# Polysketch attention with an RWKV channel mix on one core: instructions over two PSUM banks, q in rows of tokens, and a new order

## The chip, the cores and the metric

The kernel runs on one core of a Trainium2 chip. Its engines are TensorE (PE, with weight loads listed apart as PEld), VectorE (DVE), ScalarE (ACT) and GpSimd (POOL); SyncE (SP) issues transfers, and ACT can issue them too. Each engine has its own list of instructions and works through it in order; a semaphore holds an instruction until those it depends on are done. The metric is the time of one execution in device microseconds (us), as the median of several.

## The reference

```python
def phi(x):                                   # S1, S2: (8, 32)
    a = np.einsum('rd,bhsd->bhsr', S1, x)
    b = np.einsum('rd,bhsd->bhsr', S2, x)
    return np.einsum('bhsi,bhsj->bhsij', a, b).reshape(*x.shape[:-1], r * r)
q_p, k_p = phi(q), phi(k)                     # q, k, v: (4, 4, 1088, 32) fp32
kv  = np.einsum('bhsf,bhsd->bhfd', k_p, v)
z   = np.sum(k_p, axis=2)
num = np.einsum('bhsf,bhfd->bhsd', q_p, kv)
den = np.einsum('bhsf,bhf->bhs', q_p, z)[..., None] + 1e-06
x   = (num / den).transpose(0, 2, 1, 3).reshape(4, 1088, 128)

x_prev = x shifted by one token (zeros first)
xk = mu_k * x + (1 - mu_k) * x_prev
xr = mu_r * x + (1 - mu_r) * x_prev
k  = np.maximum(xk @ w_k, 0)                  # w_k: (128, 1024)
out = sigmoid(xr @ w_r) * ((k * k) @ w_v)     # w_v: (1024, 128)
```

## The kernel before

There are four batches, each with four heads of 32 channels, so that head and channel fill the 128 partitions. The steps of a batch are these, with the names and lines of the kernel before.

*k side.* `kin` arrives by a DMA (L188). DVE transposes it to `kT` (L345). PE multiplies by the sketches S1 and S2 in two groups of four matmuls, one into each of two banks (L352); DVE transposes each bank into `abT` (L363). POOL, or now and then DVE, forms the products `phk` in three parts (L370). PE sums them with `v` into one bank in 24 matmuls a third (L379 `kv`), DVE masks the result into `w` (L391), and a copy of it with its halves exchanged, `ws`, is made by a product and an ACT copy for batch 0 (L394, L396) and by two DMAs for the others.

*q side.* `qin` arrives in four DMAs, one for each head, with a descriptor of 64 floats for each two tokens (L191). DVE transposes it to `qT` in two parts, 9 and 8 of 17 token pairs (L414). For batches 0 to 2, PE expands qT by S1 and by S2 (L453 `ex`): a call fills four banks. The S1 half is copied to `a_sb` (L465, ACT or DVE), the S2 half is multiplied by it into `phq` (L471, DVE). In batch 3, the S1 side is a compact sketch instead (L427), copied to `ac` (L434), and spread by four DMAs (L441). PE then computes the denominator (L480 `den`), DVE transposes it to `dT` (L491), ACT adds the small constant (`rc`, L494), and DVE takes the reciprocal `rr` (L498) and transposes it back to `rT` (L499). The numerator (L524 `num`) fills two banks a half. In batches 0 and 3 it is copied to `r` (L533, ACT), and a product with a selection matrix spreads rT (L545 `pr`); in batches 1 and 2, rT is spread by DMAs into `r` (L506) instead. DVE multiplies both into `xT` (L557), which is x, transposed.

*Channel mix.* x is scaled by mu and by 1-mu into `y1` and `y2` (L578 ACT, or L580 DVE), in three column chunks of 384 or 320. POOL adds them to `xk` (L583) and casts x to `xbp` (L586). For each chunk PE makes eight products with w_k (L612 `up`), each in a bank; a ReLU reads the bank into `kr` (L615 ACT, or L617 DVE); `k2` is the square of two kr together (L619 DVE, or L621 ACT). PE forms the gate (L640) and the product with w_v (L645 `down`), ACT the sigmoid `sg` (L648), and DVE multiplies both to `o` (L660), which a DMA stores.

Nothing in the program decides the sequence at run time. Every step is recorded as a numbered operation in `_Plan`, and a string ORDER, written out by hand, gives the order in which they are issued. `.1` behind a number takes the operation's other engine; `*n` puts n idle matmuls ahead of it. A second string, BANKS, gives each PSUM tile one of the eight banks. In the kernel before each bank is a tile of its own:

```python
def ps(shape=(P, 512)):
    t = _Buf(psum, None, 1, list(shape), F32)
    banks.append(t)
...
for t, i in zip(banks, BANKS):
    t.tag = "bank" + i
```

Of the kernel before, what the change touches and what calls it, by code (L numbers as in the profile page):

```python
# [12 lines left out]
F32 = mybir.dt.float32  # L13
# [9 lines left out]
class _Buf:  # L23

    count = itertools.count()

# [41 lines left out]
def kernel(  # L68
# [32 lines left out]
    SWAP = (0,)  # L101
    EX = [(0, NT), (NT, HT - NT)]
# [29 lines left out]
    )  # L132
    BANKS = (
        "10320601237564456732171260706452721514346072564350474163403104553451731204621045574267462557760"
        "25730423132051303046722470571652361340720623431721132763066547546645512103661151574635771053521"
        "47770463501457403621720236421256"
# [13 lines left out]

    def ps(shape=(P, 512)):
        t = _Buf(psum, None, 1, list(shape), F32)
        banks.append(t)
        return t

# [9 lines left out]
    Sst = const.tile([R, 2, D], F32)  # L165
    idle = nc.const_aps.tensor(1.0, [P, 512], BF16)
    nc.scalar.dma_start(Sst[:, 0, :], S1)
    nc.scalar.dma_start(Sst[:, 1, :], S2)

# [30 lines left out]
    mu = const.tile([DM, 2], F32)  # L200
# [7 lines left out]
    for h in range(H):  # L208
        load_q(0, h)
# [8 lines left out]

# [3 lines left out]
    mask4 = const.tile([P, H, R], F32)  # L222
    nc.gpsimd.memset(mask4[:], 0.0)
    for h in range(H):
        nc.gpsimd.memset(mask4[32 * h:32 * h + 32, h, :], 1.0)
# [20 lines left out]
    pS = ps()  # L246
    sp_ = St[:].ap[0]
    Skb = const.tile([P, 2, H, R], F32)
# [4 lines left out]
    first_in = {nm: op("IN", 0, f"{nm}0", lambda: None) for nm in ("k", "K", "v", "q", "S")}  # L253
# [6 lines left out]
    def skb():  # L260
        nc.vector.tensor_copy(St[:].rearrange("p x r -> p (x r)"), pS[:, :2 * R])
        nc.vector.tensor_mul(Skb[:], _ap(St[:], [sp_, [R, 2], [0, H], [1, R]]),
                             _ap(mask4[:], [mask4[:].ap[0], [0, 2], [R, H], [1, R]]))
# [35 lines left out]
    o_ws = op("ACT", 64, "ws", ws, [o_sk])  # L299
    o_ska = op("POOL", 64, "ska", ska, [o_sk])  # L300
# [5 lines left out]
    IN = {("k", 0): [first_in["k"], first_in["K"]], ("v", 0): [first_in["v"]], ("q", 0): [first_in["q"]]}  # L306
    done = {}

    def arrival(nm, b):
        if (nm, b) not in IN:  # L310
            nb = len(kin) if nm == "k" else 3
            need = done[nm, b - nb] if b >= nb else []
            if nm == "k":
                IN[nm, b] = [op("SP", 544, f"k{b}", lambda: load_k(b, [0, NB]), need)] * 2
            elif nm == "q":
                IN[nm, b] = [op("SP", 136, f"q{b}", lambda h=h: load_q(b, h), need) for h in (0, 2, 1, 3)]
            else:
                IN[nm, b] = [op("SP", 136, f"v{b}", lambda g=g: load_v(b, g, nc.sync), need) for g in range(4)]
        return IN[nm, b]

    i_mu = [sync(mu[:, 0:1], moe_mu_k.rearrange("d -> d ()"), 1),
            sync(mu[:, 1:2], moe_mu_r.rearrange("d -> d ()"), 1),
            sync(wr_f[:], moe_w_r, 64)]
# [12 lines left out]
    def stage_k(b):  # L336
        kT = sb("kT", [P, NB, 32], bufs=1)
        ab = [ps() for _ in range(2)]
        abT = sb("abT", [P, 2, NT, H, R])
# [10 lines left out]
        def do_ab(x, gs):  # L350
            for g in gs:
                nc.tensor.matmul(ab[x][32 * g:32 * g + 32, :NT * 32], Skb[:, x, :, :].rearrange("p h r -> p (h r)"),  # L352
                                 fl(kT, T0[g], T0[g] + NT), start=True, stop=True)

        tt = []
        for x in range(2):
            if b == 0:
                o = [op("PE", 144, f"ab{b}", lambda x=x, i=i: do_ab(x, (2 * i, 2 * i + 1)), tr[:i + 1] + [o_sk], [kT, ab[x]],
                        stir=lambda n, x=x: stir(ab[x].t[:, 3 * P:], n, 1)) for i in range(2)]
            else:  # L360
                o = [op("PE", 288, f"ab{b}", lambda x=x: do_ab(x, range(4)), tr + [o_sk], [kT, ab[x]],
                        stir=lambda n, x=x: stir(ab[x], n))]
            tt.append(op("DVE", 288, f"abT{b}", lambda x=x: nc.vector.transpose(  # L363
                abT[:, x, :, :, :].rearrange("p t h r -> p (t h r)"), ab[x][:, :NT * 32]), o, [ab[x], abT]))

        def do_phk(engine, lo, hi):
            pp = abT[:].ap[0]
            a_bc = _ap(abT[:, 0, lo], [pp, [R, (hi - lo) * H], [1, R], [0, R]])
            b_bc = _ap(abT[:, 1, lo], [pp, [R, (hi - lo) * H], [0, R], [1, R]])
# [35 lines left out]
    def stage_q(b, w, ws_, o_w, o_s):  # L405
# [5 lines left out]
        for c0, n in EX:  # L411
            def turn(c0=c0, n=n):
                qi = qin[b % 3][:]
                nc.vector.transpose(qT[:].rearrange("p (z t) s -> p z t s", z=2)[:, :, c0:c0 + n, :],  # L414
                                    _ap(qi, [qi.ap[0], [D, 2], [2 * D, n], [1, D]], 2 * D * c0))

            done["q", b].append(op("DVE", 64 * n, f"qT{b}", turn, arrival("q", b), [qT]))

        o_a = {}
        if b >= FAR:  # L420
            pa = [ps() for _ in range(2)]
# [9 lines left out]
            oc = []  # L431
            for p in range(2):
                def keep(copy, p=p):
                    copy(ac[:, p, :], pa[p][:, :NT * 32])  # L434
# [241 lines left out]
    for t, i in zip(banks, BANKS):  # L676
        t.tag = "bank" + i
# [31 lines left out]
```

## Time and profile before

| | us |
|---|---|
| three runs | 89.41, 89.93, 96.49 (median 89.93) |
| profiled execution | 89.85, its span 88.1 |
| x of batch 0 | 22.23 to 23.68 |
| first kr (ReLU) | 27.6 |
| x of batch 1 | 39.2 to 41.7 |
| x of batch 3 | 62.33 to 63.81 |
| last kr | 81.3 |
| last o | 84.4 to 85.0 |

The lower rows are positions in the profiled span, from the trace's timeline. The profile's first part gives each engine's busy time; its windows give the same for stretches of the span, with the clock granted to TensorE; the waits name what an engine stood for; the chain follows back from the last instruction what released each step.

### The profile page before, as it was taken

To read this page: it belongs to the slowest core of one execution; us is meant where nothing else is said; L and a number is where in the kernel's file an instruction comes from. 1 tells how busy PE (TensorE), PEld (TensorE's weight loads), DVE (VectorE), ACT (ScalarE), POOL (GpSimd) and SP (SyncE) were. 2 spreads that over 40 slices of the span, in tenths; PEclk is the share of its full clock that TensorE was granted. 3 is DMA by queue.
4 is the path that set the end of the run, shared out by engine and by line. 5 is a ranking of instruction groups with operands and counts; after the bars stand their busy time and mean duration, and the time that the engine had idled before them with its cause. 6 is when DMAs were issued, how large, how long until landed. Compare 5 with 4: busy or idle time off the path is not lost.

```text
span 88.1 us, 3234 instructions
## 1 busy us (share of the span) xinstructions
PE 79.1 (90%) x1285; PEld 52.0 (59%) x1285; DVE 73.8 (84%) x166; ACT 64.4 (73%) x160; POOL 44.9 (51%) x85
## 2 busy tenths in 40 slices
PE   6994599989999999898999999989999999999930
PEld 2471377434653467455496758537668886778920
DVE  0342999998989999997959999969997999999920
ACT  2410260156399999767999999999999999999800
POOL 6850498249999999992079000590165840000000
PEclk9999999999999999999999999999999999999998
DMA  2999999999993499546797761020102041230252
GB/s 38 310 249 217 281 191 251 301 268 276 183 190 96 123 200 279 126 86 173 135 247 221 160 177 50 0 89 7 60 0 89 21 140 29 89 93 24 76 149 89
DMA packets 20464, 12.74 MB, mean 145 GB/s; under 512 B 10208, under 2 KB 19168, under 8 KB 20448
## 3 DMA queue, kind: packets, MB, share of 16 engines
q1 hardware_dynamic: 19248, 11.83, 56.2%
q10 hardware_dynamic: 1200, 0.69, 2.7%
q8 instruction: 10, 0.16, 0.9%
q14 instruction: 6, 0.05, 0.2%
HBM read 7.80 MB, written 2.23 MB: 114 GB/s over the span
## 4 chain that ended last, share of the span: by engine, by line
PE 36%; DMA 19%; DVE 16%; ACT 14%; SPq 5%; issue 5%; DVEq 0%; ACTq 0%
DMA qin<-in_q_dram 14%; ACT kr L615 9%; PE bank L645 9%; PE bank L612 8%; PE bank L453 5%; DMA a_sb<-ac 5%; PE bank L379 5%; ACT y L578 3%; DVE qT L414 3%; PE bank L524 3%; PE bank L352 2%; PE bank L640 2%; DVE abT L363 2%; DVE kr L617 2%; SPq L197 2%
## 5 line engine op out<-in xcount | busy, mean ns | idle before, releaser
L615 ACT ACTIVATE kr<-bank 128x384 bf16<-128x384 f32 (+1 forms) x73 | 30.2, 510 | 0.5 <-PE bank L612 0.2
L612 PE MATMUL bank<-xk,wk 128*128 128x384 bf16 (+1 forms) x96 | 21.5, 317 | 0.9 <-DVE xT L557 0.3
L370 POOL TENSOR_TENSOR phk<-abT 128x768 f32<-128x768 f32 x11 | 17.1, 1582 | 4.2 <-DVE abT L363 4.2
L583 POOL TENSOR_TENSOR xk<-y,y 128x384 bf16<-128x384 f32 (+1 forms) x12 | 11.9, 1005 | 13.0 <-ACT y L578 12.3
L645 PE MATMUL bank<-wv,k 128*128 128x128 bf16 x192 | 13.4, 219 | 0.1
L645 PEld LDWEIGHTS <-k 128*128 128x128 bf16 x192 | 11.8, 98 | 2.5 <-issue 1.1
L471 DVE TENSOR_TENSOR phq<-bank,a_sb 128x288 f32<-128x288 f32 (+1 forms) x32 | 12.1, 425 | 0.9 <-DMA a_sb<-ac 0.9
L453 PE MATMUL bank<-qT,WS 32*64 32x256 f32 (+1 forms) x224 | 10.6, 410 | 2.5 <-DVE qT L414 2.1
L619 DVE TENSOR_TENSOR k<-kr 128x768 bf16<-128x768 bf16 x21 | 12.8, 635 | 0.0
L617 DVE TENSOR_SCALAR kr<-bank 128x384 bf16<-128x384 f32 (+1 forms) x23 | 11.3, 521 | 0.5 <-ACT k L621 0.5
L612 PEld LDWEIGHTS <-wk 128*128 128x128 bf16 x96 | 8.1, 98 | 6.2 <-issue 3.4
L379 PEld LDWEIGHTS bank<-vt,phk 128*64 128x64 f32 x288 | 9.0, 138 | 3.2 <-POOL phk L370 1.3
L465 ACT COPY a_sb<-bank 128x288 f32<-128x288 f32 (+1 forms) x21 | 6.7, 424 | 5.6 <-PE bank L453 5.6
L379 PE MATMUL bank<-vt,phk 128*64 128x64 f32 x288 | 9.9, 224 | 0.2 <-DVE xT L557 0.2
L586 POOL CAST xbp<-xT 128x384 bf16<-128x384 f32 (+1 forms) x12 | 6.7, 581 | 5.0 <-DVE xT L557 5.0
L621 ACT ACTIVATE k<-kr 128x768 bf16<-128x768 bf16 x11 | 9.2, 904 | 0.0
L578 ACT ACTIVATE y<-xT,mu 128x384 f32<-128x384 f32 (+1 forms) x11 | 6.8, 617 | 2.8 <-DVE xT L557 2.1
L345 DVE STREAM_TRANSPOSE kT<-kin 128x1088 f32<-128x1088 f32 (+2 forms) x5 | 5.3, 1066 | 3.6 <-DMA kin<-in_k_dram 3.6
L453 PEld LDWEIGHTS bank<-qT,WS 32*64 32x64 f32 x224 | 4.2, 130 | 6.0 <-issue 2.3
L414 DVE STREAM_TRANSPOSE qT<-qin 128x512 f32<-128x512 f32 (+1 forms) x8 | 5.5, 713 | 1.9 <-DMA qin<-in_q_dram 1.9
L660 DVE TENSOR_TENSOR o<-bank,sg 128x384 f32<-128x384 f32 (+2 forms) x13 | 6.3, 496 | 0.8 <-issue 0.8
L557 DVE TENSOR_TENSOR xT<-bank,r 128x256 f32<-128x256 f32 (+1 forms) x16 | 6.2, 430 | 0.6 <-DMA r<-rT 0.5
(79 smaller groups left out, 122.3 us busy)
## 6 DMA issues: line engine op xcount, KB each, us to landing
qin<-in_q_dram SPq DMA_DIRECT2D x16, 136.0 KB, 5.2
kin<-in_k_dram SPq DMA_DIRECT2D x3, 544.0 KB, 6.0
vt<-in_v_dram SPq DMA_DIRECT2D x11, 144.0 KB, 4.9
a_sb<-ac SPq DMA_DIRECT2D x4, 288.0 KB, 4.8
out_dram<-o SPq DMA_DIRECT2D x6, 192.0 KB, 2.2
r<-rT SPq DMA_DIRECT2D x4, 144.0 KB, 4.1
xT<-in_moe_w_k_dram SPq DMA_DIRECT2D x1, 512.0 KB
wv_f<-in_moe_w_v_dram SPq DMA_DIRECT2D x1, 512.0 KB
```

The lines of the kernel that those rows point to most:

```text
L370: engine.tensor_mul(phk[:, lo:hi].rearrange("p t h i j -> p (t h) i j"), a_bc, b_bc)
L379: nc.tensor.matmul(kv[64 * u:64 * u + 64, p, :], phk[:, t, h, :, :].rearrange("p i j -> p (i j)"), _ap(vt[:, h, t, :], [pv, [(H - h) * NT ...
L453: nc.tensor.matmul(px[p][z][64 * v_:64 * v_ + 64, :n * 32], WS[32 * h:32 * h + 32, x, :], fl(qT[32 * h:32 * h + 32], t, t + n), start=True ...
L471: lambda p=p, t=t, g=g, lo=lo, pb=px[1][p][z], n=n: nc.vector.tensor_mul(fl(phq[:, p], t, t + n), pb[:, :n * 32], a_sb[:, g, p, lo:lo + n ...
L578: lambda o_, i_, m_: nc.scalar.activation(o_, i_, ACTF.Copy, scale=m_)), dep + [o_mu], [u, xT],
L583: engine.tensor_add(xk[:, c0:c0 + n], y1[:, c0:c0 + n], y2[:, c0:c0 + n])
L612: nc.tensor.matmul(kp[:, :n], wk[:, c * P:(c + 1) * P], xk[:, c0:c0 + n], start=True, stop=True)
L615: o2.append(op("ACT", n, f"kr{b}.{ci}", lambda kp=kp, kr=kr, i=i, n=n: nc.scalar.activation(kr[:, i, :n], kp[:, :n], ACTF.Relu), [o1], [kp ...
L617: alt=[("DVE", n, lambda kp=kp, kr=kr, i=i, n=n: nc.vector.tensor_scalar(kr[:, i, :n], kp[:, :n], 0.0, None, op0=ALU.max))]))
L619: ok.append(op("DVE", 2 * n, f"k2{b}.{ci}", lambda kr=kr, cc=cc, n=n, squares=squares: nc.vector.tensor_mul(squares(cc), kr[:, :, :n], kr[ ...
L621: alt=[("ACT", 2 * n, lambda kr=kr, cc=cc, n=n, squares=squares: nc.scalar.activation(squares(cc), kr[:, :, :n], ACTF.Square))]))
L645: nc.tensor.matmul(rd[:, i, :], (k2p if small else k2)[:, c, at:at + P], wv[:, c, :], start=(c == 0), stop=(c == NFF - 1))
```

## The change

- All of PSUM becomes one tile `PS` of eight banks; what was a bank's tile is an index into it. `two(pair)` describes two banks at once, with a step from the lower to the higher one. Through it one instruction reads what two read before: abT, the a copies, phq, ac, the copies of num, and kr, whose ReLU now takes two products together.
- The sketches of k are eight matmuls of 64 partitions by 32 columns in one group (mask2 in place of mask4), instead of two groups of four over 128 partitions.
- In batches 0, 1 and 2 q arrives in rows of 34 tokens: two DMAs with runs of 2304 and 2048 bytes instead of four of 256-byte runs. qT is then turned in two pieces of 256 elements a part, with a piece for the odd tokens; x is written in pairs accordingly.
- mu_k and mu_r arrive as two rows on ACT's queue at the start; a product with a small identity turns them into columns, and DVE copies these.
- The scaled x (y1, y2) is on DVE in 15 of 24 pieces, before in 3. ac is copied by DVE. Some v loads and four stores of out are issued by ACT (stores: two before).
- ORDER and BANKS are written anew. In it a good part of qT, ex and the a copies of batches 1 and 2 stands ahead of x of batch 0.

The core of the diff (line numbers of the changed kernel: two L162, q rows L205, kT L364, ab L372, abT L382, phk L390, kv L399, w L411, qT L442 and L446, ex L482, a L495, phq L505, den L514, dT L525, num L558, copies of num L569, x L582 and L609, y L636 and L638, up L669, kr L672 and L674, o L717):

```diff
+    PS = psum.tile([P, 8, 512], F32, name="banks")
+
     def ps(shape=(P, 512)):
-        t = _Buf(psum, None, 1, list(shape), F32)
+        t = _Buf(None, None, 1, list(shape), F32)
         banks.append(t)
         return t
+
+    def ps2():
+        twins.append((ps(), ps()))
+        return list(twins[-1])
+
+    def two(pair, *inner):
+        lo, hi = sorted(t.idx for t in pair)
+        return _ap(PS[:, lo, :], [PS[:].ap[0], [512 * (hi - lo), 2], *inner])
...
+    nc.scalar.dma_start(mur[0:1, :], moe_mu_k.rearrange("d -> () d"))
+    nc.scalar.dma_start(mur[1:2, :], moe_mu_r.rearrange("d -> () d"))
...
+    def load_q_rows(b, ci, queue=nc.sync):
+        lo, n = 2 * EX[ci][0], 2 * EX[ci][1]
+        queue.dma_start(qin[b % 3][:, lo:lo + n, :], q[b].rearrange("h (sp t) d -> (h sp) t d", sp=32)[:, lo:lo + n, :])
...
+    o_pmu = op("PE", 2, "pmu", lambda: nc.tensor.matmul(pmu[:, :2], mur[:], eye[:2, :2], start=True, stop=True), [first_in["M"]], [pmu])
+    o_muc = op("DVE", 2, "muc", lambda: nc.vector.tensor_copy(mu[:], pmu[:, :2]), [o_pmu], [pmu])
...
-        def do_ab(x, gs):
+        def do_ab(gs):
             for g in gs:
-                nc.tensor.matmul(ab[x][32 * g:32 * g + 32, :NT * 32], Skb[:, x, :, :].rearrange("p h r -> p (h r)"),
-                                 fl(kT, T0[g], T0[g] + NT), start=True, stop=True)
+                for p in range(2):
+                    nc.tensor.matmul(ab[p][32 * g:32 * g + 32, :NT * 32], Skb[64 * p:64 * p + 64].rearrange("p u c -> p (u c)"),
+                                     fl(kT[64 * p:64 * p + 64], T0[g], T0[g] + NT), start=True, stop=True)
...
+        def turn_ab():
+            ao = abT[:]
+            nc.vector.transpose(_ap(ao, [ao.ap[0], [4 * R, 2], [2 * R * H, NT], [1, 32]]), two(ab, [32, NT], [1, 32]))
...
+                for z in range(2):
+                    qo = qT[:, HT * z + c0:, :]
+                    nc.vector.transpose(_ap(qo, [qo.ap[0], [64, m], [1, 2], [2, 32]]),
+                                        _ap(qi, [qi.ap[0], [2 * D, m], [D, 2], [1, D]], D * (2 * c0 + 2 * m * z)))
+                if n % 2:
+                    qo = qT[:, c0 + 2 * m:, :]
+                    nc.vector.transpose(_ap(qo, [qo.ap[0], [32 * HT, 2], [1, 32]]), qi[:, 2 * c0 + 4 * m:2 * c0 + 4 * m + 2, :])
...
+                    def keep(copy, a_in=a_in, pa=px[0][p], n=n):
+                        copy(a_in(), two(pa, [1, n * 32]))
...
+                def product(p=p, a_in=a_in, pb=px[1][p], c0=c0, n=n):
+                    po = phq[:, p, c0:, :]
+                    nc.vector.tensor_mul(_ap(po, [po.ap[0], [32 * HT, 2], [1, n * 32]]), two(pb, [1, n * 32]), a_in())
...
+                o2 = [op("ACT", 2 * n, f"kr{b}.{ci}", lambda kps=kps, kr=kr, n=n: nc.scalar.activation(
+                    kr[:, :, :n], two(kps, [1, n]), ACTF.Relu), o2, kps + [kr],
+                    alt=[("DVE", 2 * n, lambda kps=kps, kr=kr, n=n: nc.vector.tensor_scalar(
+                        kr[:, :, :n], two(kps, [1, n]), 0.0, None, op0=ALU.max))])]
...
     for t, i in zip(banks, BANKS):
-        t.tag = "bank" + i
+        t.idx = int(i)
+    for a, b in twins:
+        a.idx, b.idx = sorted((a.idx, b.idx))
+    for t in banks:
+        m = t.shape[1:]
+        t.t = PS[:, t.idx, :m[0] * (m[1] if len(m) > 1 else 1)]
```

More of the change, by code (lines that the diff above doesn't have):

```diff
@@ L101 @@
     SWAP = (0,)
+    ROW = (0, 1, 2)
     EX = [(0, NT), (NT, HT - NT)]
@@ L165 @@
     Sst = const.tile([R, 2, D], F32)
+    mur = const.tile([2, DM], F32)
     idle = nc.const_aps.tensor(1.0, [P, 512], BF16)
@@ L207 @@
     load_k(0, [0, 2 * NT, NB], (nc.sync, nc.sync))
-    for h in range(H):
-        load_q(0, h)
+    assert 0 in ROW
+    for ci in range(2):
+        load_q_rows(0, ci)
     for g in (0, 1):
@@ L245 @@
     St = const.tile([P, 2, R], F32)
-    pS = ps()
+    mu = const.tile([DM, 2], F32)
+    pS, pmu = ps(), ps()
     sp_ = St[:].ap[0]
-    Skb = const.tile([P, 2, H, R], F32)
+    Skb = const.tile([P, 2, 2 * R], F32)
     SkA = const.tile([P, 2, 32], F32)
@@ L252 @@
     wr = const.tile([DM, 2, DM], BF16)
-    first_in = {nm: op("IN", 0, f"{nm}0", lambda: None) for nm in ("k", "K", "v", "q", "S")}
+    first_in = {nm: op("IN", 0, f"{nm}0", lambda: None) for nm in ("k", "K", "v", "q", "Q", "S", "M")}
     def spread_s():
@@ L314, in arrival @@
                 IN[nm, b] = [op("SP", 544, f"k{b}", lambda: load_k(b, [0, NB]), need)] * 2
+            elif nm == "q" and b in ROW:
+                IN[nm, b] = [op("SP", 64 * EX[ci][1] // 2, f"q{b}", lambda ci=ci: load_q_rows(b, ci), need) for ci in range(2)]
             elif nm == "q":
@@ L337, in stage_k @@
         kT = sb("kT", [P, NB, 32], bufs=1)
-        ab = [ps() for _ in range(2)]
-        abT = sb("abT", [P, 2, NT, H, R])
+        ab = ps2()
+        abT = sb("abT", [P, NT, H, 2, R])
         phk = sb("phk", [P, NT, H, R, R])
@@ L410, in stage_q @@
         done["q", b] = []
-        for c0, n in EX:
+        row = b in ROW
+        for ci, (c0, n) in enumerate(EX):
             def turn(c0=c0, n=n):
[L413 to L417, printed above, removed]
+                qi, m = qin[b % 3][:], n // 2
+                if not row:
+                    nc.vector.transpose(qT[:].rearrange("p (z t) s -> p z t s", z=2)[:, :, c0:c0 + n, :],
+                                        _ap(qi, [qi.ap[0], [D, 2], [2 * D, n], [1, D]], 2 * D * c0))
+                    return
+                for z in range(2):
[5 more added lines that the diff above has]
+                    nc.vector.transpose(_ap(qo, [qo.ap[0], [32 * HT, 2], [1, 32]]), qi[:, 2 * c0 + 4 * m:2 * c0 + 4 * m + 2, :])
+            done["q", b].append(op("DVE", 64 * n, f"qT{b}", turn, arrival("q", b)[ci:ci + 1] if row else arrival("q", b), [qT]))
         o_a = {}
         if b >= FAR:
-            pa = [ps() for _ in range(2)]
+            pa = ps2()
             ac = sb("ac", [P, 2, NT * 32], bufs=min(2, B - FAR))
@@ L430, in stage_q, with keep_a @@
             oa = op("PE", 288, f"ac{b}", compact, done["q", b] + [o_ska], [qT] + pa, stir=lambda n: stir(pa[0], n))
[L431 to L434, printed above, removed]
-                oc.append(op("ACT", 288, f"a{b}", lambda keep=keep: keep(nc.scalar.copy), [oa], [pa[p], ac],
-                             alt=[("DVE", 288, lambda keep=keep: keep(nc.vector.tensor_copy))]))
+            def keep_a(copy):
+                copy(ac[:], two(pa, [1, NT * 32]))
+            oc = [op("ACT", 576, f"a{b}", lambda: keep_a(nc.scalar.copy), [oa], pa + [ac],
+                     alt=[("DVE", 576, lambda: keep_a(nc.vector.tensor_copy))])]
             def spread_a(g, queue=nc.sync):
@@ L515, in stage_q @@
         for ci, (c0, n) in reversed(list(enumerate(EX))):
-            pn = [ps() for _ in range(2)]
+            pn = ps2()
             def nu(pn=pn, c0=c0, n=n):
@@ L528, in stage_q, with r_in, keep, scaled @@
                     [w, ws_, phq] + pn, stir=lambda n, pn=pn: stir(pn[0], n))
-            for z in range(2):
-                t, g = HT * z + c0, 2 * z + ci
-                if near:
-                    def keep(copy, pn=pn, z=z, t=t, n=n):
-                        copy(fl(r, t, t + n), pn[z][:, :n * 32])
-                    o_num[g] = op("ACT", n * 32, f"nc{b}", lambda keep=keep: keep(nc.scalar.copy), [on], [pn[z], r],
-                                  alt=[("DVE", n * 32, lambda keep=keep: keep(nc.vector.tensor_copy))])
-                else:
-                    o_num[g], x_in[g] = [on, o_r[g]], pn[z]
+            def r_in(c0=c0, n=n):
+                ri = r[:, c0:, :]
+                return _ap(ri, [ri.ap[0], [32 * HT, 2], [1, n * 32]])
+            if near:
+                def keep(copy, r_in=r_in, pn=pn, n=n):
+                    copy(r_in(), two(pn, [1, n * 32]))
+                o1 = op("ACT", n * 64, f"nc{b}", lambda keep=keep: keep(nc.scalar.copy), [on], pn + [r],
+                        alt=[("DVE", n * 64, lambda keep=keep: keep(nc.vector.tensor_copy))])
+                o_num[ci] = o_num[2 + ci] = o1
+            else:
+                def scaled(pn=pn, r_in=r_in, c0=c0, n=n):
+                    xo_, m = xTs[b % 2][:], n // 2
+                    if not row:
+                        nc.vector.tensor_mul(_ap(xo_, [xo_.ap[0], [1, 2], [2, n * 32]], 64 * c0), two(pn, [1, n * 32]), r_in())
+                        return
+                    for z in range(2):
+                        xi, ri = pn[z][:, :n * 32], fl(r, HT * z + c0, HT * z + c0 + n)
+                        nc.vector.tensor_mul(_ap(xo_, [xo_.ap[0], [2, m], [NB, 32], [1, 2]], 2 * c0 + 2 * m * z),
+                                             xi[:, :m * 64].rearrange("p (c s e) -> p c s e", s=32, e=2),
+                                             ri[:, :m * 64].rearrange("p (c s e) -> p c s e", s=32, e=2))
+                        if n % 2:
+                            nc.vector.tensor_mul(_ap(xo_, [xo_.ap[0], [NB, 32]], 2 * c0 + 4 * m + z), xi[:, m * 64:], ri[:, m * 64:])
+                xo[ci] = xo[2 + ci] = op("DVE", n * 64, f"x{b}", scaled, [on, o_r[ci], o_r[2 + ci], o_mu] + ([o_wk] if b == 1 else []), pn + [r, xT])
         if near:
@@ L570, in stage_m @@
             c0, n = CH[b % 2][ci]
-            dep = [xo[g] for g in range(4) if (c0 < 64 * NT if g % 2 == 0 else c0 + n > 64 * NT)]
+            dep = list(xo.values()) if b in ROW else [xo[g] for g in range(4) if (c0 < 64 * NT if g % 2 == 0 else c0 + n > 64 * NT)]
             oy[ci] = []
@@ L590, in stage_m @@
             ob[ci] = op("POOL", n, f"xb{b}.{ci}", lambda cast=cast: cast(nc.gpsimd.tensor_copy), dep, [xb_, xT],
-                        alt=[("ACT", n, lambda cast=cast: cast(nc.scalar.copy))])
+                        alt=[("ACT", n, lambda cast=cast: cast(nc.scalar.copy)), ("DVE", n, lambda cast=cast: cast(nc.vector.tensor_copy))])
         for ci in order:
```

102 lines of the change are left out of this document (50 added, 52 removed), and 48 rows, old and new, of the table ORDER.

## The prediction

> **What bounds the kernel now.** First the page's head and its chain:
>
> ```profile
> span 88.1 us, 3234 instructions
> ...
> PE 79.1 (90%) x1285; PEld 52.0 (59%) x1285; DVE 73.8 (84%) x166; ACT 64.4 (73%) x160; POOL 44.9 (51%) x85
> ...
> PE 36%; DMA 19%; DVE 16%; ACT 14%; SPq 5%; issue 5%; DVEq 0%; ACTq 0%
> ```
>
> No engine owns the end: three are full by turns, and the chain hops between them. So I look at stages (columns: window and length, busy us of PE, weight loads, DVE, ACT, POOL, granted clock, DMA share, GB/s):
>
> ```profile
> 7.00:17.00 10.00, 7.83 (x171) 4.89 (x173) 8.13 (x18) 2.22 (x7) 5.72 (x9) 1.00 1.14 239
> 17.00:27.00 10.00, 9.38 (x216) 4.85 (x208) 9.52 (x21) 6.32 (x18) 8.16 (x9) 1.00 1.05 239
> 27.00:37.00 10.00, 9.63 (x180) 5.25 (x172) 9.87 (x20) 9.74 (x24) 10.00 (x10) 1.00 0.66 160
> 37.00:47.00 10.00, 9.69 (x181) 6.52 (x180) 8.46 (x23) 8.21 (x19) 5.69 (x8) 1.00 0.70 168
> ```
>
> From 17 us on PE and DVE are busy over nine tenths, and ACT joins at 27. The kernel lives from PE, ACT and DVE working at the same time, each on PSUM banks of its own. DVE's waits:
>
> ```profile
> DVE kT L345 <- DMA kin<-in_k_dram: 3.6, 1, 3.6
> DVE qT L414 <- DMA qin<-in_q_dram: 1.9, 2, 1.7
> ```
>
> DVE has 14.3 us idle in all: 3.6 are the first load, which stays, 1.9 the q loads. Last the timeline (start, length, engine, line), which shows the overlap:
>
> ```profile
> 18.21 0.44 DVE L491 STREAM_TRANSPOSE dT<-bank 128x288 f32<-128x288 f32 x1
> ...
> 18.83 0.74 PE L453 MATMUL bank<-qT,WS 32*64 32x288 f32 x16
> ...
> 19.94 1.34 ACT L465 COPY a_sb<-bank 128x288 f32<-128x288 f32 x4
> ...
> 20.81 0.90 DVE L363 STREAM_TRANSPOSE abT<-bank 128x288 f32<-128x288 f32 x2 [0.19 <-PE bank L352]
> ```
>
> ACT copies four banks from 19.94 to 21.28 while DVE reads two others from 20.81, and neither slows the other. PE waits 0.18 us from the end of dT (18.65) to its matmul (18.83): that is a hand-over.
>
> **The change, part by part.** Paces below are from start to start of neighbours of a kind, in the same trace.
>
> *Reads of two banks.* kr (ReLU) on ACT goes at 0.371 us for 384 elements and 0.317 for 320, so 0.84 ns an element and 0.05 fixed; a pair of 384 is 0.69 instead of 0.74. DVE: 0.464 and 0.400, so 1.04 ns and 0.06 fixed; a pair is 0.86 instead of 0.93. phq, abT, a and the copies of num halve their counts too (32 to 16, 8 to 4, 24 to 12). Work saved: about 2 us on ACT, 1.5 on DVE.
>
> *Moves of work.* y moves 12 pieces from ACT (0.506 for 384) to DVE (0.328): DVE +3.7, ACT -5.7. DVE gives 8 of its 23 kr in pairs: 15x0.464+8x0.400=10.2 becomes 5x0.86+3x0.73=6.5, -3.7. ac goes from ACT to DVE, +0.66. By the sum of paces DVE stays near 69 us, ACT falls from 60 to 55 and gains some 2.4 of DMA issues (0.4 each), POOL is as before.
>
> *Sketches of k in one group.* Two groups of four matmuls at 0.67 become one of eight on half the rows. No row shows that one; the nearest is the compact q sketch, eight matmuls on 64 rows, 0.80 to 0.86, ends 0.67 and 1.34. I take 0.8: PE -0.5 a batch, -2.2 in all.
>
> *q in rows of 34 tokens.* Packets of 256 B took 18 to 24 ns each on one of 16 DMA engines, 2304 B 93 (9 times the bytes, 4 to 5 times the time). A batch was 2176x24/16=3.3 us of all engines and becomes 256x90/16=1.4. Batch 0's q is due about 2 us earlier, so the 1.7 us wait goes; next late is phk on POOL, which waits for abT and not for q. The price is an odd token: +0.2 us of qT and +0.13 of x a batch on DVE, about 1 us.
>
> *mu by a product.* Two loads of 4-byte packets leave SP (0.35 and 0.40 us of issue at 12 us), replaced by two row loads on ACT's queue at the start, one small matmul and one 0.2 us copy on DVE. These stand ahead of v's loads of ACT, 0.3 to 0.4 each; v is read by kv from 12 us and landed 5 us after issue, so I count nothing (if not covered, 0.7). The v and out issues that move to ACT cost it 0.4 each and free SP.
>
> *What comes with it.* All banks are now one PSUM tile, and a two-bank read steps from the lower to the upper bank. The compiled order of the changed kernel, with the instruction that each semaphore waits for, shows that such a read is held against everything in the banks between, reads by the other engine included. Of ACT's waits for DVE 23 of 32 are for instructions that share no bank and no tile with the waiting one; ACT for PE 10 of 48, DVE for ACT 19 of 36, DVE for PE 10 of 42, PE for ACT 26, PE for DVE 10. Before, each bank was a tile by itself and none are of this kind. A pair spans 3.6 banks on average, so nearly any two neighbours collide. The trace of before has no such wait, so each is priced by what it waits for: from nothing, where that is done anyway, to its whole rest plus a hand-over.
>
> I walk it. Up to 17.5 us (abT of batch 1, 17.48 before) I let both stand equal: the earlier q is used by the order for work of batches 1 and 2. Then, each hop with 0.15 us of hand-over:
> - ex (PE, 4 matmuls) 0.33; ACT copies banks 3 and 6, 0.53: 18.7. den writes bank 5, between, and waits: 1.05; ex 0.65; num 0.58: 21.2. ACT copies num from 1 and 6, 0.48: 21.8. Only now dT may read bank 5: 0.36, 22.3. Before it ended at 18.65.
> - k sketches behind dT 0.8, num 0.6, phq over banks 0 and 7 (held by that num) 0.66, abT 0.66, rr and rT 0.8, four qT pieces 1.3, x of batch 0 1.7: 29.3. Before: 23.68.
> - kv meanwhile; w 0.19: 30.0. ACT's copy of 1 and 6 waits for w in bank 2: 0.53. ex 16 matmuls 1.3. Copies on ACT 0.48 and, held by that, on DVE 0.6; two phq 1.2: 34.6. kv, ex, den 2.5: 37.3. dT; two copies 1.0 (held by dT); ex 0.65; phq 0.6; up 0.33 (held by phq): the first kr starts at 40.9. Before: 27.6.
> - From there to x of batch 1: seven kr pairs and between them, one at a time, kv 0.83, phq 0.6, qT, k2 and w 1.3, k sketches 0.8, q sketches 0.8, up, abT 0.66, ex 0.65, ac 0.66, num 0.6, num 0.58, phq 0.6, gate and up 0.5, phq 0.6, x 1.7. With the pairs, 16 us of work and 23 hand-overs: about 60. Before, x of batch 1 ended at 41.7 with 12 kr done; here 14 (7 pairs) are.
>
> So up to x of batch 1 some 18 us are lost. For the rest before took 88.1-41.7=46 us. The same walk goes on less tightly (channel mix has no long dependences): 18th pair at 83, x of batch 3 at 92.7 (62.3 before), the end at 128, which is 68 us. The bounds are 46, if no such wait costs anything there, and 68; the walk's hops are nearer to the upper, and I take 63: a span of 123. Around the span lie 89.85-88.1=1.75 us (the profiled run stands 0.1 under the median of 89.93): **125 us**.
>
> Downward: the walk's hand-overs, if free, take some 6 us off up to 60, which with the 46 gives 54+46+1.75=102. Upward: 128+1.75 is 130, and a hand-over is 0.18 in the row above, not 0.15, and lengths run 0.08 to 0.15 over pace (dT 0.44 against 0.36), up to 8 us more: 138.
>
> **Rivals.**
> *A, the gain.* The banks' waits are met by instructions already done, as nearly all hand-overs between 17 and 37 us before were. Then only work counts: 88.1 less the 1.9 of q waits and 1.2 of PE's 2.2 (the rest beside DVE) is 85.0, 86.8 us with what lies around. For it speaks that the totals fall on PE and ACT and hold on DVE; against it dT of batch 0, 3.6 us late by two waits alone. It decides at 3.1 us: where these waits cost the critical engine less than that, the kernel is not slower, under 1.3 us it is faster by 2%. [...]
> *B, the waits eat just the gain*: 3.1 us of loss, 88 to 91. It needs 15 of the walk's 18 us to be covered by other work; but each engine runs its list in order, and what stands behind a waiting head covers nothing.
> *C, half covered*: 2 to 10 of the 18 us are lost and nothing after them, 92 to 100.
> *D, PE slows too.* PEclk is 1.00 in all these windows, with PE nine tenths busy. In the walk PE is about half busy. The longest gap I find is 2.5 us (32.1 to 34.6). If the clock halved for a fifth of 67 us of PE work, 13 us more: 138 to 145. [...]
>
> **How the numbers follow.** Forecast (102 to 138) 0.78, A 0.10, B 0.04, C 0.05, D 0.03. From 96 to 138 A, B, D and half of C are left out, 0.2. Two percent, 1.8 us, is about what a measurement here can tell from none: faster only with A, 0.10; same with B, 0.04; slower with the rest, 0.86.
>
> **What would show it.** Right: DVE near 55% busy, ACT under 50%; waits of ACT for DVE and of DVE for ACT in the list with whole microseconds, where before's is under one; dT of batch 0 ending at about 22, x of batch 0 near 29, first kr near 41, x of batch 1 near 60. The saved work seen beside it: kr pairs on ACT about 0.7 apart, one k sketch group of 0.8, q of batch 0 landed before 7 us. Wrong: dT before 19.5 us and a first kr before 30 mean A or B; a granted clock under 1.0 in the middle means D; x of batch 1 at 60 but the end by 108 means that only the rest was overestimated.

## The result and the profile after

The changed kernel took 153.05 us (median of four runs, 150.19 to 156.27) against 90.0 before: 1.68 times as long (95% interval 1.655 to 1.707). Two executions of the changed kernel were slower than the others (153.82 and 156.27 us, at granted clocks of 0.796 and 0.745), so the ratio is that of the faster runs alone (150.19 and 152.28 us, at 0.814 and 0.805, 151.2 in the mean), while the profile below is of the run of 153.82 us. The direction was as forecast, and so was its first mechanism, waits for banks between; the size was not: 125 was forecast, with a range up to 138.

The head of the profile after (busy time by engine), the clock granted to TensorE in 40 slices, and the shares of the chain that ended last:

```profile
span 152.0 us, 3142 instructions
...
PE 103.2 (68%) x1279; PEld 59.5 (39%) x1280; DVE 75.9 (50%) x155; ACT 61.8 (41%) x102; POOL 45.7 (30%) x85
...
PEclk9999986978659568555599857789955569999999
...
PE 57%; ACT 17%; DVE 14%; issue 5%; DMA 4%; ACTq 1%; SPq 0%; DVEq 0%
```

DVE and ACT do about the work that they did before (75.9 and 61.8 us against 73.8 and 64.4), in a span longer by 64 us. PE has two new traits: its matmuls are busy 103 us where they were 79, and its clock is no longer full (0.796 in the mean, 0.997 before).

The waits of ACT, then of DVE, in the changed kernel (us in total, times, longest):

```profile
ACT kr L672 <- PE banks L669: 16.9, 11, 3.4
...
ACT a_sb L495 <- DVE dT L525: 6.5, 1, 6.5
...
ACT a_sb L495 <- DVE w L411: 5.2, 1, 5.2
ACT kr L672 <- DVE kr L674: 5.1, 3, 2.2
```

```profile
DVE phq L505 <- ACT kr L672: 6.7, 1, 6.7
...
DVE dT L525 <- ACT r L569: 5.1, 1, 5.1
```

The first row is in part the ReLU's wait for its own products. In the other rows the two instructions need nothing of each other: a copy of the expanded q has nothing to do with a denominator or a masked state, nor phq with a ReLU; what joins them is a bank between the two of the wide read. Before, ACT waited for DVE in two places only, for the x that it scales and for the sketches at the start:

```profile
ACT y L578 <- DVE xT L557: 2.1, 1, 2.1
...
ACT WS L270 <- DVE St L261: 1.8, 1, 1.8
```

The timeline of the changed kernel where the walk began (start, length):

```profile
19.99 0.75 PE L482 MATMUL banks<-qT,WS 32*64 32x288 f32 x16 [1.91 <-DVE abT L382]
...
20.77 1.18 ACT L495 COPY a_sb<-banks 128x576 f32<-128x576 f32 x2 [2.38 <-PE banks L482]
21.46 0.48 PE L514 MATMUL banks<-phq,w 128*32 128x288 f32 x2 [0.73 <-ACT a_sb L495]
...
23.34 1.26 PE L482 MATMUL banks<-qT,WS 32*64 32x288 f32 x16
...
25.58 0.59 ACT L569 COPY r<-banks 128x512 f32<-128x512 f32 x1 [3.63 <-PE banks L558]
26.20 0.48 DVE L525 STREAM_TRANSPOSE dT<-banks 128x288 f32<-128x288 f32 x1 [5.07 <-ACT r L569]
```

The hops come in the order of the walk: abT, half of ex, the copy of banks 3 and 6, den behind it, ex, num, the copy of num over banks 1 to 6, and only then dT, 2.8 us after den's last matmul. But den lasts 1.9 us and ex 1.26, which the walk had at 1.05 and 0.65.

### The profile page after: what moved, and what is told of

The parts are those of the page before. It is cut to its first block, busy times and chain, and to the rows that moved or that the text cites. A ratio compares the mean times of both kernels' runs of the same rounds, so it can differ in the third digit from the quotient of the medians.

```text
span 152.0 us, 3142 instructions
## 1 busy us (share of the span) xinstructions
PE 103.2 (68%) x1279; PEld 59.5 (39%) x1280; DVE 75.9 (50%) x155; ACT 61.8 (41%) x102; POOL 45.7 (30%) x85
## 3 DMA queue, kind: packets, MB, share of 16 engines
q1 hardware_dynamic: 12784, 11.54, 29.3%
## 4 chain that ended last, share of the span: by engine, by line
PE 57%; ACT 17%; DVE 14%; issue 5%; DMA 4%; ACTq 1%; SPq 0%; DVEq 0%
ACT kr L672 12%; PE banks L669 10%; PE banks L702 10%; PE banks L399 8%; PE banks L482 6%; PE banks L558 6%; PE banks L514 5%; PE banks L697 4%; DVE phq L505 3%; DVE kr L674 3%; PE banks L372 3%; ACT a_sb L495 2%; DMA qin<-in_q_dram 2%; DMA mur<-in_moe_mu_r_dram 2%; PE banks L309 2%
## 5 line engine op out<-in xcount | busy, mean ns | idle before, releaser
L672 ACT ACTIVATE kr<-banks 128x768 bf16<-128x768 f32 (+1 forms) x40 | 30.1, 777 | 41.7 <-PE banks L669 16.9
L669 PE MATMUL banks<-xk,wk 128*128 128x384 bf16 (+1 forms) x96 | 27.7, 372 | 18.4 <-ACT kr L672 11.5
L390 POOL TENSOR_TENSOR phk<-abT 128x768 f32<-128x768 f32 x11 | 16.3, 1506 | 23.9 <-DVE abT L382 23.9
L505 DVE TENSOR_TENSOR phq<-banks,a_sb 128x576 f32<-128x576 f32 (+1 forms) x16 | 11.4, 719 | 22.6 <-PE banks L558 7.9
L482 PE MATMUL banks<-qT,WS 32*64 32x288 f32 (+1 forms) x224 | 12.7, 507 | 8.2 <-DVE abT L382 2.9
L669 PEld LDWEIGHTS <-wk 128*128 128x128 bf16 x96 | 9.2, 109 | 22.3 <-issue 17.8
L399 PE MATMUL banks<-vt,phk 128*64 128x64 f32 x288 | 13.1, 261 | 5.0 <-issue 2.9
L399 PEld LDWEIGHTS banks<-vt,phk 128*64 128x64 f32 x288 | 11.9, 172 | 10.1 <-issue 9.1
L495 ACT COPY a_sb<-banks 128x576 f32<-128x576 f32 (+1 forms) x11 | 6.6, 616 | 22.5 <-PE banks L482 10.8
L702 PE MATMUL banks<-wv,k 128*128 128x128 bf16 x192 | 14.8, 231 | 1.4 <-DVE kr L674 1.4
L717 DVE TENSOR_TENSOR o<-banks,sg 128x384 f32<-128x384 f32 (+2 forms) x13 | 6.5, 503 | 8.8 <-PE banks L702 6.8
L558 PE MATMUL banks<-phq,w 64*32 64x256 f32 (+1 forms) x64 | 8.3, 613 | 3.3 <-ACT kr L672 1.9
L674 DVE TENSOR_SCALAR kr<-banks 128x768 bf16<-128x768 f32 (+1 forms) x8 | 7.2, 904 | 6.2 <-PE banks L702 3.9
L482 PEld LDWEIGHTS banks<-qT,WS 32*64 32x64 f32 x224 | 4.3, 157 | 14.3 <-DVE abT L382 4.3
L514 PE MATMUL banks<-phq,w 128*32 128x288 f32 x32 | 7.6, 625 | 2.0 <-ACT kr L672 1.3
L697 PE MATMUL banks<-wr,xbp 128*128 128x128 bf16 x72 | 7.7, 262 | 1.7 <-DVE kr L674 1.0
L558 PE MATMUL banks<-phq,ws 64*32 64x256 f32 (+1 forms) x64 | 8.3, 612 | 0.0
```

What stands on the lines that cost most here:

```text
L390: engine.tensor_mul(phk[:, lo:hi].rearrange("p t h i j -> p (t h) i j"), a_bc, b_bc)
L399: nc.tensor.matmul(kv[64 * u:64 * u + 64, p, :], phk[:, t, h, :, :].rearrange("p i j -> p (i j)"), _ap(vt[:, h, t, :], [pv, [(H - h) * NT ...
L482: nc.tensor.matmul(px[p][z][64 * v_:64 * v_ + 64, :n * 32], WS[32 * h:32 * h + 32, x, :], fl(qT[32 * h:32 * h + 32], t, t + n), start=True ...
L505: nc.vector.tensor_mul(_ap(po, [po.ap[0], [32 * HT, 2], [1, n * 32]]), two(pb, [1, n * 32]), a_in())
L514: nc.tensor.matmul(pd[32 * g:32 * g + 32, :NT * 32], wz[g // 2][:, p, 32:], phq[:, p, TD[g]:TD[g] + NT, :].rearrange("p t s -> p (t s)"), ...
L558: nc.tensor.matmul(pn[z][32 * h:32 * h + 32, :n * 32], wz[z][rs, p, :32], phq[rs, p, t:t + n, :].rearrange("p t s -> p (t s)"), start=True ...
```

## The experiments

Is it the span of the wide reads, their width, or the order? And what is the clock's part? A read's *banks between* are those from its lower to its upper bank, without the two; over the 89 pairs of banks in the changed kernel they sum up to 217. (Four pairs, those of num in batches 1 and 2, are still read bank by bank, so 85 instructions read two banks at once, with 207 banks between.)

**Banks renamed.** Only the number of each bank changes: 0 to 7 become 1, 6, 4, 3, 2, 7, 5, 0 (the two tiles of a pair can change places, since the first always takes the lower number).

```diff
-        "21034175670213456072563561345340161651257732710415650342156264402361270437163405251504130617465"
+        "46132607501463275104753756327321656576470034061267571324675452214356401230653217476712631560257"
...
```

> The changed kernel with its eight banks renamed by one fixed permutation; order, instructions and which tile follows which in a bank stay. Only the number of banks that lie between the two of a pair changes: 113 in sum over the 89 pairs instead of 217. Theory (reads over two banks wait for what lies between, and the idle PE then gets a lower clock): about half of the 63 us of loss goes, 110 to 135 us, the granted clock over 0.85. Rival 1 (the wide instructions themselves, being longer, make others wait) and rival 2 (the new order is bad): nothing that they blame is changed, 148 to 156 us.

113.15 us. With every instruction and its place unchanged, 40 of the 63 us are gone. From the profile of this kernel:

```profile
PE 81.0 (73%) x1280; PEld 50.3 (46%) x1280; DVE 76.5 (69%) x155; ACT 61.0 (55%) x102; POOL 45.1 (41%) x85
...
PEclk9999999999999999999999999999999999999999
```

Width and order are as in the changed kernel, so neither alone can have made these 40 us. The clock of this execution is full, and the same matmuls are busy 81 us, not 103, so the 40 us hold the waits and the slow clock together.

**All pairs neighbours.** BANKS is given out anew so that no bank lies between.

```diff
-        "21034175670213456072563561345340161651257732710415650342156264402361270437163405251504130617465"
+        "67045030123546712543267610103520322345546321341054077612453204541671032456754012304567325456456"
...
```

> The changed kernel with banks given out anew so that all 89 pairs are neighbours and no bank lies between; order and instructions as in the changed kernel. Theory: waits between instructions without a common bank vanish, 84 to 92 us (the gain case of the prediction was 86.8), granted clock 0.98 or more, x of batch 1 before 42 us. Rival 1 (width): 140 us or more, since every instruction is as wide as before. Rival 2 (order): 140 us or more.

94.95 us, 1.052 of before (1.023 to 1.082), clock 0.98, x of batch 1 done at 43.8. So 58 us go with the banks between. It is above the expected band, and slower than before, not faster; x of batch 1 is late too (before 42 was expected).

**One bank an instruction**, with order and banks of the changed kernel:

```diff
-                copy(ac[:], two(pa, [1, NT * 32]))
+                for i in range(2):
+                    copy(_ap(ac[:], [ac[:].ap[0], [1, NT * 32]], NT * 32 * i), bank_of(pa, i, [1, NT * 32]))
```

and likewise for abT, a, phq, num's copies and kr.

> The changed kernel with its order and its banks, where every instruction over two banks is issued as two over one bank each. Theory: no read spans a bank, so 86 to 95 us; against reads of neighbouring banks it pays the fixed parts of some 89 more instructions, 0.05 us each on ACT and 0.06 on DVE. Rival 1 (width): as fast as that too. Rival 2 (order): 140 us or more.

91.26 us, 1.019 of before (0.994 to 1.045). All of the change but its wide reads costs some 2 us, by the interval between nothing and 4; the wide reads cost the other 60. Of the foreign waits none is left: DVE no longer waits for ACT, and ACT waits for DVE once, for the sketches at the start.

```profile
ACT WS L290 <- DVE St L282: 2.2, 1, 2.2
```

**Neighbouring banks, one bank an instruction**: both edits together.

> The banks of the neighbouring-pairs kernel, every instruction over two banks issued as two. Against that kernel this isolates what the merging of instructions is worth when it costs no wait: by the fixed parts (0.05 us on ACT, 0.06 on DVE, some 60 and 29 instructions) 3 us of ACT and 1.7 of DVE; with DVE the fuller engine I expect 1 to 3 us slower than the kernel with neighbouring pairs. If merging were worth nothing: the same within 1%.

94.25 us, 1.050 (1.031 to 1.068): as the kernel that merges them. The two profiles, merged first:

```profile
PE 79.4 (86%) x1280; PEld 50.0 (54%) x1280; DVE 74.3 (80%) x155; ACT 60.6 (65%) x102; POOL 45.6 (49%) x85
```

```profile
PE 79.8 (86%) x1280; PEld 50.8 (55%) x1280; DVE 76.6 (83%) x185; ACT 63.3 (69%) x157; POOL 45.5 (49%) x85
```

Merging takes 2.3 us off DVE and 2.7 off ACT, much as its fixed parts said, and nothing off the time. The two kernels with neighbouring banks lie 3 us above the one with the change's own banks: which tile follows which in a bank also counts. I moved that without knowing the times, so it says nothing against neighbours as such.

**Idle matmuls**, added to the changed kernel ahead of products for which TensorE stood still.

```diff
-        ... 36 166 21 37 168 52 291 ...
+        ... 36 s5*7 166 21 37 168 s0*2 52 291 ...
```

A word `sK*n` puts n idle matmuls of 512 columns into bank K.

> The changed kernel, its order, banks and wide reads kept, with idle matmuls put ahead of 31 products for which TensorE stood still (93 times 512 columns, 22 us at full clock, into banks that nobody uses then). They add work and take no wait away. Theory (the clock follows how busy TensorE is, and halved matmuls are part of the chain): the granted clock goes from 0.80 to over 0.95 and the time falls to 125 to 140 us although work is added; the hand walk at full clock was 130. Rival (the low clock is a sign of waiting and not a cause of time, or the matmuls' lengths don't lie on the path): the time stays at 148 or more, or grows by up to 20 us.

146.07 us at a clock of 0.94: 5 us less than the 151.2, with 22 us of work more, but short of the expected band. The idle matmuls filled the waits badly. They write a bank too, and stood some 21 us themselves, nearly always for the last read of that bank, where before the products behind them had stood; only then did they run. The longest row of theirs is this one:

```profile
PE banks L313 <- ACT kr L677: 9.3, 10, 1.3
```

To see what the clock goes with I cut the changed kernel's trace at the points where its clock steps, which lie 3.41 us or a multiple of it apart (window and length; busy PE, weight loads, DVE, ACT, POOL; granted clock; DMA):

```profile
18.31:21.72 3.41, 1.00 (x20) 0.40 (x24) 2.82 (x6) 1.03 (x3) 1.70 (x2) 1.00 1.04 271
21.72:25.14 3.42, 3.42 (x48) 0.98 (x40) 0.00 (x0) 0.23 (x1) 2.73 (x2) 0.50 0.56 164
25.14:28.55 3.41, 2.19 (x48) 0.50 (x32) 1.48 (x3) 0.95 (x2) 0.00 (x0) 1.00 0.00 0
28.55:31.96 3.41, 1.69 (x44) 1.14 (x44) 3.14 (x8) 1.18 (x2) 2.16 (x2) 1.00 0.01 2
31.96:35.38 3.42, 3.42 (x50) 2.67 (x52) 1.64 (x6) 0.00 (x0) 1.25 (x2) 0.50 0.02 5
```

PE busy for 1.00 of 3.41 us, then half clock; 3.42 of 3.42 at half clock, then full; 2.19, and full again; 1.69, and half. The next run puts idle matmuls only where a window was under 0.55 busy, the one after it adds ten.

```diff
-        ... 36 166 21 37 168 52 291 ... 65 282 69 ...
+        ... 36 s5*4 166 21 37 168 52 291 ... 65 s7*6 282 69 ...
```

> The changed kernel with idle matmuls at 18 places (38 times 512 columns, some 9 us), only in those stretches of 3.4 us in which TensorE was busy for less than 0.55 of the time; the earlier run had 93 at 31 places and most of them ran over the wait that they were to fill. Theory (half clock follows a stretch with less than half of it busy, and costs time): granted clock 0.90 or more, 134 to 145 us. Rival (the 7 us of the earlier run came from something else): 148 us or more.

143.94 us at 0.93, in the expected band: 7 us less than the 151.2, with fewer of them.

> The changed kernel with idle matmuls at 22 places (48, some 11 us): those of the run with 38, and ten more where a stretch of 3.4 us was still busy for less than half. Theory (half clock follows such a stretch): four of its seven half-clock stretches go, granted clock 0.95 or more, 138 to 143 us. Rival (what was won is all there is, more idle matmuls only delay): 144 us or more, whatever the clock.

145.85 us, the middle of 147.91 at a clock of 0.90 and 143.79 at 0.94; the run before had 144.15 and 143.73, both at 0.93. The ten added idle matmuls won nothing: the profiled execution, that of 147.91 us, had a lower clock than either of the run before, and the other took as long as the faster of those. The median is the rival's number, and how much the clock costs stays between bounds (below).

**Which wide reads.** Only kr wide, then all but kr wide, with order and banks of the changed kernel. The second has, in place of the wide ReLU:

```diff
+                    for i in range(2):
+                        if act:
+                            nc.scalar.activation(kr[:, i, :n], bank_of(kps, i, [1, n]), ACTF.Relu)
+                        else:
+                            nc.vector.tensor_scalar(kr[:, i, :n], bank_of(kps, i, [1, n]), 0.0, None, op0=ALU.max)
```

and the first has this loop's like everywhere else.

> The changed kernel with its order and banks, where only kr, the ReLU, still reads two banks at once (48 of the 89 pairs); abT, a, phq, ac and the copies of num are issued one bank at a time. Theory (by the walk, the attention's wide reads cost some 14 us up to the first kr, the rest from then on through both): x of batch 0 and the first kr as in the one-bank kernel (about 25 and 32 us), the loss from there on, 105 to 130 us. Rival (the attention's wide reads alone do the harm): under 96 us.

125.65 us (126.59 and 124.71). x of batch 0 ends at 28.6, the first kr starts at 34.0, against 26.6 and 31.8 with one bank an instruction: some 2 us later, and most of the loss follows behind. From its waits:

```profile
DVE phq L513 <- ACT kr L681: 8.1, 3, 3.7
...
DVE abT L387 <- ACT kr L681: 3.5, 1, 3.5
```

> The counterpart of the run with only the ReLU wide: in the changed kernel kr reads one bank at a time, abT, a, phq, ac and the copies of num read two. Theory (both kinds of wide read wait for foreign banks; the ReLU alone cost 34 of 62 us): a loss of 12 to 35 us, 102 to 126 us; x of batch 0 as late as in the changed kernel within 3 us (30 to 35 us). Rival (the ReLU's reads do all of it, the others only wait behind them): under 96 us.

114.97 us (117.84, which is the profiled run, and 112.09); x of batch 0 ends at 36.7 and the first kr starts at 50.2, about as late as in the changed kernel (34.9 and 49.5). From its waits:

```profile
ACT a_sb L499 <- DVE dT L529: 6.5, 1, 6.5
ACT a_sb L499 <- DVE w L415: 5.9, 1, 5.9
```

The ReLU alone costs 125.65-91.26=34 us, the others alone 24, by the lower of their two runs 33 and 21. In sum that is 54 to 58 of some 60, so the two losses nearly add up. The delay up to the first kr is the attention's own.

**Where the gains went.** In the one-bank kernel PE's longest wait is this:

```profile
PE banks L320 <- DMA mur<-in_moe_mu_r_dram: 1.4, 1, 1.4
```

The product for mu stands ahead of the sketches' spread, and its rows come late.

```diff
-        "... 5 0 24 14 1 3 ... 26*8 27 15 38 ..."
+        "... 5 0 24 1 3 ... 26*8 27 14 15 38 ..."
```

> The kernel with the changed order and banks and one-bank instructions (91.3 us), where the small product for mu is issued right before its copy instead of ahead of the sketches' spread. There TensorE stood 1.4 us for mu's rows, and the k sketches began at 6.62 us instead of 5.70. Theory (this wait lies on the prologue's chain): 0.5 to 1 us faster, 90.3 to 90.8. Rival (POOL's phk or the load of k sets the prologue's end): no difference, 91.0 to 91.5.

90.47 us, 0.998 of before (0.991 to 1.004); the one-bank kernel was 1.019 (0.994 to 1.045). The medians differ by the 0.8 us that was expected, but they were taken on two chips, and the intervals overlap: that the product cost time is likely and not shown.

Next, with that, banks renamed so that 40 of the 89 pairs are neighbours, and those alone read by one instruction (36, as four of the 40 are read bank by bank anyway):

```diff
+    def pieces(pair):
+        return [None] if abs(pair[0].idx - pair[1].idx) == 1 else [0, 1]
```

> As the kernel with mu late, but the banks renamed by a permutation that makes 40 of the 89 pairs neighbours, and those 40 read by one instruction; the other 49 by two. No read spans a foreign bank. Theory (merging saves its fixed parts, 0.05 to 0.06 us a pair, some of it with DVE full): 40 pairs are worth about 2.2 us of ACT and DVE together, 0.5 to 1.5 us of time: 89 to 90.5, level with before. Rival (merging is worth nothing, since a pair waits for the later of its two products): as with mu late, or up to 1 us slower.

89.82 us, 0.980 of before (0.971 to 0.988). A second time:

> The hybrid kernel again, in more rounds. It measured 0.980 of before (0.971 to 0.988). If that holds: 0.97 to 0.99. If it was the luck of that chip: 0.99 to 1.01.

91.2 us, 0.996 (0.991 to 1.001). The first gain did not hold on this second chip; the hybrid is level with before or one or two per cent ahead. Its DVE still waits 1.1 us for mu's product:

```profile
DVE mu L329 <- PE banks L328: 1.1, 1, 1.1
```

So the product was moved behind abT of batch 0.

```diff
-        "... 26*8 27 14 15 38 273 28 13 152 ..."
+        "... 26*8 27 38 273 28 14 15 13 152 ..."
```

> The hybrid kernel, where the product for mu and its copy are issued behind abT of batch 0. In the hybrid VectorE stood 1.1 us for that product, ahead of the first transpose of q (6.53 us). Theory (mu's product still costs the prologue, and the prologue sets the rest): 0.5 to 1.1 us faster than the hybrid, which measured 0.980 and 0.996 of before: 0.975 to 0.985. Rival (q arrives no earlier, or phk on GpSimd ends the prologue): 0.985 to 1.0.

89.69 us, 0.988 (0.980 to 0.995), between the hybrid's two results, and in the rival's band. It is 1.2% better than before, by its interval between half a per cent and two, which is under the 2% that the prediction calls telling, and it can't be told from the hybrid. The wait moved on: DVE then waited 1.3 us and 1.2 us for q.

**q by token pairs again**, in the hybrid.

```diff
-    ROW = (0, 1, 2)
+    ROW = ()
...
-    for ci in range(2):
-        load_q_rows(0, ci)
+    for h in range(H):
+        load_q(0, h)
```

> The hybrid kernel (changed order, renamed banks, neighbouring pairs read at once) with q of batches 0 to 2 loaded by token pairs as before the change: 256-byte runs, one transpose a part, x of batches 1 and 2 written in one piece a half; two loads of batches 1 and 2 are issued one place earlier, since the first transpose now needs all heads. Theory of the prediction (rows save the 1.7 us wait for q of batch 0, and cost 0.33 us a batch on VectorE): 0.7 to 2 us slower than the hybrid. Rival (the order fills the wait anyway, or POOL's phk ends the prologue): within 0.5 us of it.

97.7 us, 1.091 of before (1.083 to 1.098); the hybrid was 0.980 and 0.996. This is far more than the 0.7 to 2 us expected:

```profile
DVE qT L453 <- DMA qin<-in_q_dram: 9.1, 3, 6.7
```

The new order asks for q of batch 1 ahead of the masked state of batch 0, and by pairs it isn't there: DVE waits from 14.9 to 21.6 us and makes w only at 22.9. Behind that wait the clock is at half: the 16 matmuls of ex take 1.26 us at 24.00 and at 27.27, as in the half-clock window of the changed kernel (0.74 in the kernel before), and a mean clock of 0.947 over 96.2 us is that of half clock for some 10 us. The rows are worth 6.5 us or more in this order, not the 1.7 us that the old order waited.

## Why the prediction was wrong, and where it was right

The forecast's first mechanism stands: reads over two banks wait for the banks between, and less of that gives less time (217 banks: 153 us; 113: 113; none: 95; with the change's own banks read one at a time: 91). The time was 28 us more than forecast, 15 above the range.

**The failed step: the walk prices every PE hop at full clock.** The slow clock was put aside as rival D. That found no gap above 2.5 us in the walk, and got a chance of 0.03 beside the forecast, as though the two excluded each other. They don't: the walk leaves PE "about half busy", and in the changed kernel's trace the clock fell to half eight times, each time after a window of 3.41 us in which PE was busy for 0.30 to 0.50 of it, with a longest single gap of 1.0 to 2.3 us. The clock was 0.80, and its fall in the middle was the sign that the prediction gave for D. The effect has bounds. The same 1280 matmuls are busy 103.2 us here and 79.4 with neighbouring pairs, so about 24 us at most are slow matmuls. Idle matmuls, which add work and take away no wait, won some 7 us (1.61 of before against 1.68), so about that at least. What it is exactly stays open: I found no way to hold the clock full without delaying something. D's own time, 138 to 145, came nearer than the forecast, and was still 8 us short; its chance was wrong, and half clock for a fifth of PE's work was an estimate that no window of before shows.

**The walk.** Its hops are those of the trace, and its places were late by a growing amount:

| | forecast | measured |
|---|---|---|
| abT of batch 1 (end) | 17.5 | 19.9 |
| dT of batch 0 (end) | 22.3 | 26.7 |
| x of batch 0 (end) | 29.3 | 34.9 |
| first kr (start) | 40.9 | 49.5 |
| x of batch 1 (end) | 60 | 74.5 |
| end | 123 | 152.0 |

Of the 4.4 us that dT is late, 2.4 are there where the walk begins (the next point has 0.9 of them, the rest isn't shown), and 1.5 come from den and ex at half clock (1.9 and 1.26 us instead of 1.05 and 0.65). The estimate from x of batch 1 to the end was 63, measured 77.5. The walk's own end, 128 at full clock, would have been the better term than 123; taking part of it off was a mistake of direction. In windows of half clock PE was busy for 27.3 us up to x of batch 1 and for 21.2 behind it. Half of that, 13.6 and 10.6 us, is the most that the clock can have added; the walk's places were late by 14.5 there (2.4 of them from the start), and by 9.5 more behind (77.5 against 68). So with the 24 us taken off 152 is 128 too, but each is an upper bound, and the agreement proves little.

**mu by a product: "I count nothing (if not covered, 0.7)".** Not covered: PE waited 1.3 us for the rows of mu in the changed kernel (1.4 in the one-bank kernel), and the sketches of k began at 6.59 us instead of 5.70. Those 0.9 us are part of the 2.4 above; the walk's assumption that both stand equal at 17.5 was wrong.

**Paces and sums were nearly right.** A k sketch group took 0.72 us at full clock (at 16.95 in the changed kernel; 0.8 taken). DVE was to stay level and ACT to fall by 5 us: busy times were 2.1 us over before's and 2.6 under, with neighbouring pairs 0.5 over and 3.8 under. (DVE's own two paces, 0.464 and 0.400, give 1.00 ns an element and not 1.04; a pair changes by 0.01 us.) q of batch 0 was transposed from 6.23 us on (8.88 before; "landed before 7 us").

**Rival A** fell, as its weight said: without foreign waits the change is at 0.98 to 1.05 of before, not at 86.8 us. It had counted the whole of the q wait and half of PE's saving as time; in the hybrid mu's product, dT and q's later parts are waited for instead. In the row at 19.94 of the prediction ACT and DVE read different banks at the same time: the four copies last 0.44 to 0.47 us each and the two abT 0.48, against 0.40 to 0.51 and 0.44 to 0.48 elsewhere in that kernel. It did not help the changed kernel, where a semaphore holds such reads back though their banks differ (a copy on ACT for 6.5 us, until dT).

**Rows of q** were priced by the wait of the old order; by the new order they were worth about four times that, or more.

## What to carry to other kernels

A view that steps over part of a tile can be ordered against all that lies between its ends: read the waits of the compiled program for instructions that share no data, before believing a saving in instruction counts (here a copy on ACT stood 6.5 us for a transpose of another bank). Widen an instruction only where its banks are neighbours, and price it by what its longer wait delays; here 85 merged reads took 5 us off two engines and nothing off the time. Price a drop in TensorE's busy share twice, for the waits and for the clock: here the share went from 90 to 68% and the mean clock from 0.997 to 0.796.

## What the runs showed of the hardware that was not expected

In the trace of the changed kernel the stretches of full and of half clock begin and end at points that lie 3.41 us or a multiple of it apart; a window is here the 3.41 us from one such point to the next. From 11.48 us, where the record of the clock begins, to 148.02, behind which PE has next to no work, there are 40 windows. I compared each one's busy share of PE with the next one's clock. Full clock fell to half after eight windows, with PE busy for 0.30 to 0.50 of the time and a longest gap of 1.0 to 2.3 us. It stayed full after 14: thirteen with 0.53 or more busy, and one with 0.49 (137.78 to 141.19 us). From half it came back after eight windows with 0.89 or more busy (at half clock, where a matmul lasts longer: the 16 of ex 1.26 us instead of 0.75), and stayed at half after ten: nine with 0.74 or less, and one with 0.96 (59.27 to 62.68 us). In the kernel before the clock is full from 5.61 us, where its record begins, to 87.5, and in the windows of 3.41 us up to 84.1 PE is busy for 0.58 or more. This is what two traces show. At which share the clock falls in other kernels they don't show, nor why one window with 0.49 busy was followed by full clock and three with 0.49 to 0.50 by half.

Over whole spans, PE was busy 73% at a mean clock of 1.00 in the profiled run of the renamed kernel, 86% at 0.98 with neighbouring pairs, and 68% at 0.80 in the changed kernel.
